# Attention layer, forward and gradients in one kernel: pairs of heads from head 32, eight fixed slot pairs and staging in single slots

## The chip, the cores and the metric

The kernel runs on one core of one Trainium2 chip. The metric is the device time of one execution in microseconds; the median of three runs before the change is 1707.09 us (1704.97 to 1707.36).

## What is computed

One decode step of a pre-LayerNorm block (cached attention, then a SwiGLU), and the gradients of its output for all inputs. B = 4 tokens, 32 heads, 4096 cached keys of 128 numbers; all tensors are bfloat16.

```python
def _A_ref(x, k_cache, v_cache, wq, wo):
    q = (x @ wq).reshape(B, Sq, H, Dh).transpose(0, 2, 1, 3)
    scores = jnp.einsum("bhqd,bhkd->bhqk", q, k_cache) * (Dh ** -0.5)
    p = _softmax(scores, axis=-1)
    o = jnp.einsum("bhqk,bhkd->bhqd", p, v_cache)
    return o.transpose(0, 2, 1, 3).reshape(B, Sq, H * Dh) @ wo
def _B_ref(x, w1, w3, w2):
    return (_silu(x @ w1) * (x @ w3)) @ w2

h = x + _A_ref(_layernorm(x), k_cache, v_cache, wq, wo)
h2 = h + _B_ref(_layernorm(h), w1, w3, w2)
# outputs: h2 and the gradients for x, k_cache, v_cache, wq, wo, w1, w3, w2
```

With 128 pairs of token and head, K, V, dK and dV have 134 MB each. For one query per head the gradients of the caches are outer products: dV = p dO^T and dK = dS q^T, with dS = p (V dO - c) / sqrt(128), where c is the product of dO and o. So the kernel reads K once, reads V twice (once for o, once more for V dO), writes dK and dV once, and does the small weight gradients beside it.

## The kernel before

The order of all instructions is written out by hand. Each engine works through its own instructions in that order, and all large transfers are issued by SyncE (SP), also in order.

**Slots.** Nearly all data goes through one SBUF tile, `arena`, cut into 23 slots of 4160 bfloat16 numbers per partition (`NSLOT`, `SLOT`). A head of K, V, dK or dV fills one slot (1 MB). `Slot` takes the slot that has been free longest (`free`, a queue); `give` puts it back when the code that used it has been written out. What then really waits on the chip is the next user of that slot: a load waits for the engines that read the old contents, and a computation that writes the slot waits for the store from it to land. `Slot2` takes two neighbouring slots for a pair of heads (2 MB, 16 KB per partition). In the last part of the kernel (`part["B"]`) `lone_slot` picks single slots at the ends of odd runs of free slots, and `Slot2.choices` lists the neighbouring pairs that are free in runs.

**Forward part.** By groups of two heads: scores, softmax, and a matrix from which o and part of dq come; K and V are loaded a few heads ahead. Eight slots, M, keep results of all 128 heads for the backward part. After it a short middle part does the SwiGLU forward and backward and loads V again, as many heads as slots are free.

**Backward part.** First heads one by one, from head `SP` = 24 in pairs of heads.
- `front(s)` (singles) and `front_pair(t)` (pairs): V is transposed by TensorE in groups of eight 128x128 blocks (L803, L1274) and evicted by ScalarE (L804, L1275) onto the same slot; matmuls with dO (L1208, L1289) give dP. After a group of heads `rows_out` and `rows_T` turn the result around, and `group_dS` or `group_dS_pair` (L1302, L1305, VectorE) makes dS.
- `grad_V`, `grad_K` (L820, L1232) and `grad_pair` (L1355, L1365): VectorE writes the outer product into a fresh slot or pair (2.3 us for a head at L809, 4.4 us for a pair at L1355), and SP stores it.
- `load_V2` (L836) and `load_pair` (L1257) load V ahead: `load_pairs` keeps up to three pairs loaded and not yet used. dV runs eight heads ahead of dK (`lead_V`), V's transposes three pairs ahead (`LP`).
- `side(s)` puts small work between the heads: up to head 20 what is left of dO (`rest_of_dO`), up to head 34 `dq_work`, which gives back an M slot after each 16 heads, and from head 35 two steps of `side_work` per head.
- `side_work` makes dq and dx (loading wq again by `load_wq2`), then the gradient of wq, then loads w2, makes the output h2 (its rows are put into slots `rows1`, `rows2`: ScalarE copies at L1096, a VectorE addition at L1111), and then the gradients of w2, w1, w3 and wo. A weight gradient is built by `grad_unit`: one matmul of 512 columns into PSUM, evicted by ScalarE at the next unit (L979).
- `staged` collects these units in a pair of slots and stores the pair (L1071) when it is full: seven stores of 1.8 or 2 MB. Halfway through a pair it takes the next one, so that for half of the time two pairs are held for staging.

The heart of the single and paired choice before the change:

```python
def __init__(self, name, src=free):          # Slot
    if src is free and part["B"]:
        lone_slot()
    self.i = src.popleft()
```

Of the kernel before, what the change touches and what calls it, by code (L numbers as in the profile page):

```python
# [18 lines left out]
NSLOT = 23  # L19
JQ = 8  # L20
NPE = 1
SP = 24


@with_exitstack
def kernel(
# [22 lines left out]
    nc = tc.nc  # L49
    P = nc.NUM_PARTITIONS  # L50

    B = A_x.shape[0]
    D = A_x.shape[-1]
    H = A_k_cache.shape[1]
    Sk = A_k_cache.shape[2]
    Dh = A_k_cache.shape[3]
    F = B_w1.shape[1]
    NH = B * H
    HD = H * Dh
    assert NH == P and Dh == P and H == 32 and Sk == 32 * P  # L60
    assert D == 4 * P and F % P == 0
    DC = D // P
    SJ = Sk // P
    FC = F // P
# [12 lines left out]
    f_chunks = []  # L77
# [27 lines left out]
    fcon = cF.enter_context(tc.tile_pool(name="fcon", bufs=1))  # L105

    free = deque(range(NSLOT))
    part = {"B": False}
    arena = slotp.tile([P, NSLOT * SLOT], BF16, name="arena")

    class Slot:
        def __init__(self, name, src=free):
            if src is free and part["B"]:
                lone_slot()
            self.i = src.popleft()
            self.t = arena[:, self.i * SLOT:(self.i + 1) * SLOT]

        def b(self, n=4096):
# [8 lines left out]
        def give(self):  # L127
            free.append(self.i)

    def runs_of_free():  # L130
        runs = []
        for i in sorted(free):
            if runs and runs[-1][-1] == i - 1:
                runs[-1].append(i)
            else:
                runs.append([i])
        return runs

    def lone_slot():
        at = {i: n for n, i in enumerate(free)}  # L140
        runs = runs_of_free()
        odd = [e for r in runs if len(r) % 2 for e in (r[0], r[-1])]
        i = min(odd or [e for r in runs for e in (r[0], r[-1])], key=lambda e: at[e])
        free.remove(i)
        free.appendleft(i)

    class Slot2:
        @staticmethod
        def choices():
            at = {i: n for n, i in enumerate(free)}  # L150
            return [(max(at[r[n]], at[r[n + 1]]), r[n]) for r in runs_of_free() for n in range(len(r) - 1)
                    if len(r) % 2 or n % 2 == 0]

        def __init__(self):
            self.i = min(self.choices())[1]
# [55 lines left out]
    for i in range(2):  # L211
        t = fcon.tile([P, 64], BF16, name=f"onesw{i}")
# [4 lines left out]
    def ones_window(col):  # L217
# [11 lines left out]
                          in_=rowg[:, None, :, None].to_broadcast([P, 4, 8, 4]))  # L229
# [70 lines left out]
    with ExitStack() as c0:  # L300
# [19 lines left out]
        for r in range(2):  # L320
            for t_ in range(2):
                for q in range(4):
                    nc.tensor.matmul(qr_ps[32 * q:32 * (q + 1), 2 * r + t_, :], lhsT=ident_b[:, 64 * r + t_:64 * (r + 1):2],
                                     rhs=qT_bf[:], start=True, stop=True, tile_position=(0, 32 * q))
# [204 lines left out]
    def two_slots(nm):  # L529
        return [Slot(nm + "a"), Slot(nm + "b")]  # L530
# [7 lines left out]
    def load_w2():  # L538
        sl = two_slots("w2")
        for i in range(2):  # L540
            nc.sync.dma_start(out=sl[i].b(7 * D).rearrange("p (c j) -> p c j", c=7),
                              in_=B_w2.rearrange("(p c) j -> p c j", c=FC)[:, i * 7:(i + 1) * 7, :])
        return sl
# [93 lines left out]
    units = {"d": d_hh_units()}  # L637
# [15 lines left out]
    for gi in range(NGI):  # L653
        nxt = gi < NGI - 1
        a, na, nb = gi * G, gi * G + 2, gi * G + 3
# [137 lines left out]
    V2s, VTs = {}, {}  # L793
# [38 lines left out]
    def load_V2(eng=nc.sync):  # L832
        s = nv["next"]
        if s < SP:
            V2s[s] = Slot("V2", vring if vring else free)
            eng.dma_start(out=V2s[s].heads(), in_=cache_head(A_v_cache, s))  # L836
            nv["next"] += 1

    with ExitStack() as cm:
# [70 lines left out]
        for sl in w1 + w3:  # L910
            sl.give()
        rs = Slot("reps")
        rep_bufs = {nm_: [rs.b()[:, (2 * k + i) * 512:(2 * k + i + 1) * 512].rearrange("p (i d) -> p i d", i=REP) for i in range(2)]
                    for k, nm_ in enumerate(("rq", "rdo"))}
        dh = rs.f(2080)[0:B, 1024:1024 + D]
# [50 lines left out]
    with ExitStack() as c2:  # L966
# [9 lines left out]
        def grad_flush():  # L976
            if gu:
                dst, ps, n = gu.pop()
                nc.scalar.copy(out=dst, in_=ps[:, 0:n])  # L979


        def grad_unit(dst, lhsT, rhs):
            n = rhs.shape[-1]
            ps = psg.tile([P, 512], FP32, tag="gps", name="gps")
            nc.tensor.matmul(ps[:, 0:n], lhsT=lhsT, rhs=rhs, start=True, stop=True)
            grad_flush()
            gu.append((dst, ps, n))
# [23 lines left out]
        def side_work():  # L1011
# [4 lines left out]
            t = rs.f(2080)[:, 1536:1536 + NH]  # L1016
# [6 lines left out]
            flat = Slot("dqflat")  # L1023
# [7 lines left out]
            for cc in range(DC):  # L1031
                wq2 = wq2s.popleft()
# [19 lines left out]
            xhat_bf = fs.t[0:B, 6 * D:7 * D]  # L1052
# [5 lines left out]
            nc.vector.tensor_tensor(out=dx_bf, in0=dh, in1=lnbx, op=ALU.add)  # L1058
            nc.gpsimd.dma_start(out=o1_2, in_=dx_bf)
            yield  # L1060
            stage = deque([Slot2()])

            def staged(units, out_ap):
                st = stage.popleft()
                for n, (a, w_, lhsT, rhs) in enumerate(units):
                    if n == len(units) // 2:
                        stage.append(Slot2())
                    grad_unit(st.t[:, a:a + w_], lhsT, rhs)
                    yield
                grad_flush()  # L1070
                nc.sync.dma_start(out=out_ap, in_=st.t[:, 0:out_ap.shape[-1]])  # L1071
                st.give()

            for i in range(2):
                if i == 1:
                    w2 = load_w2()
                yield from staged([(r * HD + n8 * 512, 512, xhat_bf[0:B, 2 * P * i + r:2 * P * (i + 1):2],
                                    flat.b(HD)[0:B, n8 * 512:(n8 + 1) * 512]) for r in range(2) for n8 in range(HD // 512)],
                                  out_4[2 * P * i:2 * P * (i + 1), :].rearrange("(p r) n -> p (r n)", r=2))
            flat.give()  # L1080
            fs.give()

            r1, r2 = Slot("rows1"), Slot("rows2")
            hh_rows, dg_rows, du_rows = r1.t[0:B, 0:F], r1.t[0:B, F:2 * F], r2.t[0:B, 0:F]
            gr_bf, dh_bf, hhat_bf = r1.t[0:B, 2 * F:2 * F + D], r2.t[0:B, F:F + D], r2.t[0:B, F + D:F + 2 * D]
# [21 lines left out]
            for sl in w2:  # L1107
# [3 lines left out]
            nc.vector.tensor_tensor(out=h2_bf, in0=hrows, in1=o2_ps[0:B, :], op=ALU.add)  # L1111
            nc.gpsimd.dma_start(out=o0_2, in_=h2_bf)
            yield
            hw = hh_rows.rearrange("b (p k) -> b k p", k=FC)
            yield from staged([(k * D, D, hw[:, k, :], gr_bf) for k in range(FC)],
                              out_8.rearrange("(p k) j -> p (k j)", k=FC))
            oflat = Slot("oflat")
            for b in range(B):
                nc.gpsimd.dma_start(out=oflat.b(HD)[b:b + 1, :], in_=O_sb[b::B, :])
            nw = hhat_bf.rearrange("b (p k) -> b k p", k=DC)  # L1120
            for (rows, out_ap) in ((dg_rows, out_6), (du_rows, out_7)):
                yield from staged([(k * F + f0_, w_, nw[:, k, :], rows[:, f0_:f0_ + w_]) for k in range(DC) for (f0_, w_) in f_chunks],
                                  out_ap.rearrange("(p k) f -> p (k f)", k=DC))
            r1.give()
            for h0 in range(0, H, 16):
                ow = oflat.b(HD)[0:B, h0 * P:(h0 + 16) * P].rearrange("b (p k) -> b k p", k=16)
                yield from staged([(k * D, D, ow[:, k, :], dh_bf) for k in range(16)],
                                  out_5[h0 * P:(h0 + 16) * P, :].rearrange("(p k) j -> p (k j)", k=16))
            stage.popleft().give()
            oflat.give()  # L1130
            r2.give()

        units["s"] = side_work()


# [29 lines left out]
        rows = {}  # L1165
# [5 lines left out]
        def dO_window(s):  # L1171
            if s < SP:
                nc.gpsimd.tensor_copy(out=zd[s % B][:, 32:132:67], in_=dOT_bf[:, s:s + 1].to_broadcast([P, 2]))

        def P_pairs(s):
            if s < SP and s not in P2s:
                P2s[s] = bw3.tile([P, SJ, 2], BF16, tag="P2", name="P2")
                nc.gpsimd.tensor_copy(out=P2s[s][:], in_=P_all[:, s, :, None].to_broadcast([P, SJ, 2]))
# [13 lines left out]
        def front(s):  # L1192
# [20 lines left out]
            sl = VTs.pop(s)  # L1213
            (vring if nv["next"] < SP and len(V2s) + len(VTs) + len(vring) < NV2 else free).append(sl.i)

# [19 lines left out]
        def prefetch():  # L1235
            while nv["next"] < SP and vring:
                load_V2(nc.sync)


        NT = (NH - SP) // 2  # L1240
        H0 = SP // B
        pV, pP2, pdS, psl = {}, {}, {}, {}
        npv = {"next": 0}
# [9 lines left out]
        def load_pair():  # L1253
            t = npv["next"]
            npv["next"] += 1
            pV[t] = Slot2()
            nc.sync.dma_start(out=pV[t].t[:, 0:2 * SJ * Dh], in_=two_heads(A_v_cache, t))  # L1257

        def load_pairs(t):
            while npv["next"] < NT and (npv["next"] <= t or len(pV) < 3 and len(Slot2.choices()) > 1):  # L1260
                load_pair()

        def dO_pair(t):
# [44 lines left out]
        Pp, zt, P2b = {}, [], []  # L1308
# [189 lines left out]
```

## Time and profile before

| | |
|---|---|
| span of the profiled execution | 1707.2 us |
| busy: PE, DVE, ACT, POOL | 73%, 72%, 56%, 18% |
| bytes moved, mean rate | 707.45 MB, 414 GB/s |
| read from HBM, written to HBM | 422.59 MB, 282.34 MB |
| stores of 2 MB, median time to landing | 108, 21.2 us |
| loads of V by pairs, median time to landing | 52, 24.6 us |
| matmul clock granted, mean | 0.845 |

A reader of this profile should look at stretches of time and not at totals. The shares of PE, DVE and ACT are averages over a forward part (to about 655 us), a middle part (to about 715 us) and a backward part, which use the engines differently; the rate of the DMA engines in 40 slices shows where the transfers run at their best and where they do not. "Time to landing" is the time from a transfer's issue until its last piece has arrived, so it includes the time spent in the queue: a long one means that much work stands in front of it. A wait in the waits view names the engine and line that waited, what it waited for, and then the microseconds in total, the number of waits and the longest.

### The profile page before, as it was taken

To read this page: it belongs to the slowest core of one execution; us is meant where nothing else is said; L and a number is where in the kernel's file an instruction comes from. 1 tells how busy PE (TensorE), PEld (TensorE's weight loads), DVE (VectorE), ACT (ScalarE), POOL (GpSimd) and SP (SyncE) were. 2 spreads that over 40 slices of the span, in tenths; PEclk is the share of its full clock that TensorE was granted. 3 is DMA by queue.
4 is the path that set the end of the run, shared out by engine and by line. 5 is a ranking of instruction groups with operands and counts; after the bars stand their busy time and mean duration, and the time that the engine had idled before them with its cause. 6 is when DMAs were issued, how large, how long until landed. Compare 5 with 4: busy or idle time off the path is not lost. (4 is left out here: it accounts for less than half of the span.)

```text
span 1707.2 us, 37798 instructions
## 1 busy us (share of the span) xinstructions
PE 1247.2 (73%) x16232; PEld 959.9 (56%) x16232; DVE 1232.0 (72%) x1190; ACT 958.9 (56%) x1489; POOL 314.0 (18%) x575
## 2 busy tenths in 40 slices
PE   5889888888888888878776666577557665766642
PEld 4777776767676767656565555445334443444431
DVE  5989999999999986667396665665555565555574
ACT  3555444544454444676576576567557665756541
POOL 1211222223222321223003020012103011011010
PEclk9999999999999999798888788866668666767685
DMA  9999999999999999999999999999999999999997
GB/s 401 424 425 424 424 423 425 424 424 423 414 423 412 424 406 401 379 424 425 421 375 427 428 425 428 429 429 430 427 413 428 412 411 403 407 413 406 399 402 336
DMA packets 78264, 707.45 MB, mean 414 GB/s; under 512 B 8444, under 2 KB 12680, under 8 KB 14224
## 3 DMA queue, kind: packets, MB, share of 16 engines
q1 hardware_dynamic: 77680, 704.94, 99.1%
q8 instruction: 127, 2.08, 0.5%
q14 instruction: 41, 0.34, 0.0%
q0 software_dynamic: 416, 0.10, 0.0%
HBM read 422.59 MB, written 282.34 MB: 413 GB/s over the span
## 5 line engine op out<-in xcount | busy, mean ns | idle before, releaser
L1275 ACT COPY arena<-pt_tps 128x1024 bf16<-128x1024 bf16 x416 | 400.4, 1023 | 243.3 <-PE pt_tps L1274 243.0
L1274 PE MATMUL pt_tps<-ident_b,arena 128*128 128x128 bf16 x3328 | 333.9, 272 | 220.8 <-DMA arena<-in_A_v_cache_dram 148.8
L1274 PEld LDWEIGHTS <-arena 128*128 128x128 bf16 x3328 | 288.0, 126 | 323.7 <-DMA arena<-in_A_v_cache_dram 174.6
L1355 DVE TENSOR_TENSOR arena<-arena 128x8192 bf16<-128x8192 bf16 x52 | 229.9, 4421 | 163.4 <-DMA out_dram<-arena 161.9
L1355 DVE TENSOR_TENSOR arena<-dS,arena 128x8192 bf16<-128x8192 bf16 x52 | 230.0, 4426 | 131.8 <-DMA out_dram<-arena 131.8
L475 PE MATMUL M_ps<-arena 128*128 128x130 bf16 x4096 | 286.6, 222 | 37.5 <-DMA arena<-in_A_v_cache_dram 37.1
L460 DVE TENSOR_TENSOR arena<-arena 128x4096 bf16<-128x4096 bf16 x128 | 292.5, 2285 | 24.9 <-POOL arena L456 24.9
L475 PEld LDWEIGHTS <-arena 128*128 128x128 bf16 x4096 | 253.8, 99 | 58.4 <-DMA arena<-in_A_v_cache_dram 50.5
L367 DVE STREAM_TRANSPOSE arena<-arena 128x512 f32<-128x512 f32 (+1 forms) x321 | 250.6, 797 | 0.0
L362 ACT COPY arena<-pt_tps 128x1024 bf16<-128x1024 bf16 x128 | 129.4, 1012 | 186.8 <-PE pt_tps L361 150.3
L1352 POOL COPY arena<-arena 128x128 bf16<-128x128 bf16 x52 | 71.5, 1376 | 598.2 <-DVE arena L1355 380.8
L373 POOL TENSOR_TENSOR W<-qrep,wmask 128x128 bf16<-128x128 bf16 x128 | 120.5, 941 | 85.6 <-PE S_ps L393 70.7
L456 POOL COPY arena<-P_all 128x64 bf16<-128x64 bf16 x128 | 32.4, 253 | 413.8 <-ACT P_all L450 410.8
L804 ACT COPY arena<-pt_tps 128x1024 bf16<-128x1024 bf16 x96 | 91.7, 1026 | 18.3 <-PE pt_tps L803 17.0
L1289 PE MATMUL dP_ps<-arena 128*32 128x512 bf16 x832 | 92.2, 474 | 9.8 <-ACT arena L1275 9.5
L450 ACT COPY P_all<-pt_P 32x64 bf16<-32x64 bf16 x256 | 51.9, 203 | 55.3 <-PE pt_P L446 53.0
L803 PE MATMUL pt_tps<-ident_b,arena 128*128 128x128 bf16 x768 | 64.2, 242 | 24.6 <-ACT arena L804 20.4
L361 PE MATMUL pt_tps<-ident_b,arena 128*128 128x128 bf16 x1024 | 80.5, 223 | 0.0
L485 PE MATMUL kP_ps<-arena,onesw 128*32 128x512 bf16 x1024 | 79.2, 386 | 0.0
L809 DVE TENSOR_TENSOR arena<-dS,arena 128x4096 bf16<-128x4096 bf16 x24 | 55.0, 2297 | 30.2 <-DMA out_dram<-arena 29.9
L361 PEld LDWEIGHTS <-arena 128*128 128x128 bf16 x1024 | 62.0, 100 | 25.9 <-issue 25.8
L393 PE MATMUL S_ps<-arena,W 128*32 128x256 bf16 x1536 | 75.2, 285 | 0.5 <-DVE arena L367 0.2
(245 smaller groups left out, 1503.4 us busy)
## 6 DMA issues: line engine op xcount, KB each, us to landing
out_dram<-arena SPq DMA_DIRECT2D x108, 2048.0 KB, 21.2
arena<-in_A_v_cache_dram SPq DMA_DIRECT2D x152, 1024.0 KB, 15.7
arena<-in_A_k_cache_dram SPq DMA_DIRECT2D x128, 1024.0 KB, 15.5
arena<-in_A_v_cache_dram SPq DMA_DIRECT2D x52, 2048.0 KB, 24.6
out_dram<-arena SPq DMA_DIRECT2D x48, 1024.0 KB, 12.5
arena<-in_A_wq_dram SPq DMA_DIRECT2D x8, 1024.0 KB, 18.0
arena<-in_B_w_dram SPq DMA_DIRECT2D x8, 896.0 KB, 15.2
out_dram<-arena SPq DMA_DIRECT2D x3, 1792.0 KB, 25.2
```

The costliest lines, as they stand in the source:

```text
L361: nc.tensor.transpose(pt[:, i, :], Kn[:, c * GW + i, :], ident_b[:])
L362: nc.scalar.copy(out=KT[:, c * GW:(c + 1) * GW, :], in_=pt[:])
L367: nc.vector.transpose(out=KT[:, c * w_:(c + n) * w_], in_=Kn[:, c * w_:(c + n) * w_])
L373: nc.gpsimd.tensor_tensor(out=W[:, hl], in0=qrep[:, :, s:s + 1].to_broadcast([P, 4, 32]), in1=wmask[:, hl, None, :].to_broadcast([P, 4, 32 ...
L460: nc.vector.tensor_tensor(out=PK[:, :, 0:Dh].rearrange("p j (r t) -> p j r t", t=2), in0=Ks[s].heads().rearrange("p j (r t) -> p j r t", t=2),
L475: nc.tensor.matmul(hold["M"][:], lhsT=Vn[:, j, :], rhs=PK[:, j, :], start=(j == 0), stop=(j == SJ - 1))
L485: nc.tensor.matmul(hold["kP"][32 * q:32 * (q + 1), :, :], lhsT=ones_window(w), rhs=PK[:, j0:j0 + 4, 0:Dh], start=(w == 0 and c == 0), stop ...
L804: nc.scalar.copy(out=v[:, g * GW:(g + 1) * GW, :], in_=pt[:])
L1274: nc.tensor.transpose(pt[:, i, :], v[:, g * GW + i, :], ident_b[:])
L1275: nc.scalar.copy(out=v[:, g * GW:(g + 1) * GW, :], in_=pt[:])
L1289: nc.tensor.matmul(rows["acc"][32 * c:32 * (c + 1), :], lhsT=zt[t % B][:, 32 - m:64 - m], rhs=v[:, j0:j0 + 4, :], start=(pl == 0 and u == ...
L1355: nc.vector.tensor_tensor(out=dst.rearrange("p (j r t) -> p j r t", r=Dh // 2, t=2), in0=col2[:, :, None, :].to_broadcast([P, 2 * SJ, Dh / ...
```

## The change

1. Pairs begin at head 32 instead of 24 (`SP`), so the backward part has 48 pairs and not 52.
2. After the slot `reps` is taken, the first eight even-aligned slot pairs that do not hold it are fixed as `part["pairs"]`. Pairs for V, dV and dK come only from these, until the side work is done; then from all aligned pairs. `runs_of_free` and `lone_slot` go.
3. The slots of side work (`SIDE`: P by pairs, wq, dq, rows, o, staging) come from the seven slots outside the fixed pairs.
4. Weight gradients are staged in one slot each: 14 stores of 0.9 or 1 MB. The layout of the rows in DRAM changes with it: 7 or 8 KB in one piece per partition.
5. w2 is loaded after the gradient of wq and not in its middle. `load_pairs` counts single V heads that are loaded too.

The purpose is that the pairs that carry the large transfers are never taken for staging, and that pairs begin when the M slots have been given back.

```diff
-SP = 24
+SP = 32
+NPAIR = 8
...
-    part = {"B": False}
+    part = {"B": False, "side_done": False}
+    SIDE = ("Pp", "wq2", "dqflat", "fin", "rows1", "rows2", "oflat", "w2a", "w2b", "gwq", "gw2", "gw13", "gwo")
...
-            if src is free and part["B"]:
-                lone_slot()
-            self.i = src.popleft()
+            if name in SIDE and part["B"]:
+                self.i = next(i for i in free if i not in part["pairs"])
+                free.remove(self.i)
+            else:
+                self.i = src.popleft()
...
-            return [(max(at[r[n]], at[r[n + 1]]), r[n]) for r in runs_of_free() for n in range(len(r) - 1)
-                    if len(r) % 2 or n % 2 == 0]
+            return [(max(at[i], at[i + 1]), i) for i in (range(0, NSLOT - 1, 2) if part["side_done"] else sorted(part["pairs"])[::2])
+                    if i in at and i + 1 in at]
...
         rs = Slot("reps")
+        kept = [i for i in range(0, NSLOT - 1, 2) if rs.i not in (i, i + 1)][:NPAIR]
+        part["pairs"] = {j for i in kept for j in (i, i + 1)}
...
-            stage = deque([Slot2()])
-
-            def staged(units, out_ap):
-                st = stage.popleft()
-                for n, (a, w_, lhsT, rhs) in enumerate(units):
-                    if n == len(units) // 2:
-                        stage.append(Slot2())
-                    grad_unit(st.t[:, a:a + w_], lhsT, rhs)
+            for cc in range(DC):
+                st = Slot("gwq")
+                for n8 in range(HD // 512):
+                    grad_unit(st.b(HD)[:, n8 * 512:(n8 + 1) * 512], xhat_bf[0:B, cc * P:(cc + 1) * P],
+                              flat.b(HD)[0:B, n8 * 512:(n8 + 1) * 512])
                     yield
                 grad_flush()
-                nc.sync.dma_start(out=out_ap, in_=st.t[:, 0:out_ap.shape[-1]])
+                nc.sync.dma_start(out=out_4[cc * P:(cc + 1) * P, :], in_=st.b(HD))
                 st.give()
...
             flat.give()
             fs.give()
+            w2 = load_w2()
...
+            part["side_done"] = True
...
-            while npv["next"] < NT and (npv["next"] <= t or len(pV) < 3 and len(Slot2.choices()) > 1):
+            while npv["next"] < NT and (npv["next"] <= t or len(V2s) + 2 * len(pV) < 6 and len(Slot2.choices()) > 1):
```

The staging loops of the gradients of w2 (two slots), w1 and w3 (two each) and wo (four) are changed in the same way as that of wq (four).

More of the change, by code (lines that the diff above doesn't have):

```diff
@@ L128, in give @@
             free.append(self.i)
[L130 to L145, printed above, removed]
     class Slot2:
@@ L1060, in side_work @@
             yield
-            stage = deque([Slot2()])
-            def staged(units, out_ap):
-                st = stage.popleft()
-                for n, (a, w_, lhsT, rhs) in enumerate(units):
-                    if n == len(units) // 2:
-                        stage.append(Slot2())
-                    grad_unit(st.t[:, a:a + w_], lhsT, rhs)
+            for cc in range(DC):
[3 more added lines that the diff above has]
+                              flat.b(HD)[0:B, n8 * 512:(n8 + 1) * 512])
                     yield
                 grad_flush()
-                nc.sync.dma_start(out=out_ap, in_=st.t[:, 0:out_ap.shape[-1]])
+                nc.sync.dma_start(out=out_4[cc * P:(cc + 1) * P, :], in_=st.b(HD))
                 st.give()
[L1074 to L1079, printed above, removed]
             flat.give()
             fs.give()
+            w2 = load_w2()
             r1, r2 = Slot("rows1"), Slot("rows2")
@@ L1113, in side_work @@
             yield
-            hw = hh_rows.rearrange("b (p k) -> b k p", k=FC)
-            yield from staged([(k * D, D, hw[:, k, :], gr_bf) for k in range(FC)],
-                              out_8.rearrange("(p k) j -> p (k j)", k=FC))
+            for i in range(2):
+                st = Slot("gw2")
+                hw = hh_rows[:, i * 7 * P:(i + 1) * 7 * P].rearrange("b (p k) -> b k p", k=7)
+                for k in range(7):
+                    grad_unit(st.b(7 * D)[:, k * D:(k + 1) * D], hw[:, k, :], gr_bf)
+                    yield
+                grad_flush()
+                nc.sync.dma_start(out=out_8[i * 7 * P:(i + 1) * 7 * P, :].rearrange("(p c) j -> p c j", c=7),
+                                  in_=st.b(7 * D).rearrange("p (c j) -> p c j", c=7))
+                st.give()
             oflat = Slot("oflat")
@@ L1119, in side_work @@
                 nc.gpsimd.dma_start(out=oflat.b(HD)[b:b + 1, :], in_=O_sb[b::B, :])
-            nw = hhat_bf.rearrange("b (p k) -> b k p", k=DC)
             for (rows, out_ap) in ((dg_rows, out_6), (du_rows, out_7)):
-                yield from staged([(k * F + f0_, w_, nw[:, k, :], rows[:, f0_:f0_ + w_]) for k in range(DC) for (f0_, w_) in f_chunks],
-                                  out_ap.rearrange("(p k) f -> p (k f)", k=DC))
-            r1.give()
[L1125 to L1129, printed above, removed]
+                for i in range(2):
+                    st = Slot("gw13")
+                    nw = hhat_bf[0:B, i * 2 * P:(i + 1) * 2 * P].rearrange("b (p k) -> b k p", k=2)
+                    for k in range(2):
+                        for (f0_, w_) in f_chunks:
+                            grad_unit(st.b(2 * F)[:, k * F + f0_:k * F + f0_ + w_],
+                                      nw[:, k, :], rows[:, f0_:f0_ + w_])
+                            yield
+                    grad_flush()
+                    nc.sync.dma_start(out=out_ap[i * 2 * P:(i + 1) * 2 * P, :].rearrange("(p c) f -> p c f", c=2),
+                                      in_=st.b(2 * F).rearrange("p (c f) -> p c f", c=2))
+                    st.give()
+            r1.give()
+            for h0 in range(0, H, 8):
+                st = Slot("gwo")
+                ow = oflat.b(HD)[0:B, h0 * P:(h0 + 8) * P].rearrange("b (p k) -> b k p", k=8)
+                for k in range(8):
+                    grad_unit(st.b(8 * D)[:, k * D:(k + 1) * D], ow[:, k, :], dh_bf)
+                    yield
+                grad_flush()
+                nc.sync.dma_start(out=out_5[h0 * P:(h0 + 8) * P, :].rearrange("(p k) j -> p k j", k=8),
+                                  in_=st.b(8 * D).rearrange("p (k j) -> p k j", k=8))
+                st.give()
             oflat.give()
             r2.give()
+            part["side_done"] = True
         units["s"] = side_work()
```

## The prediction

> **What bounds the kernel now.** I read the page's parts 2 and 3 first. DMA is the only row that is full in every slice, and one queue holds it.
>
> ```profile
> DMA  9999999999999999999999999999999999999997
> GB/s 401 424 425 424 424 423 425 424 424 423 414 423 412 424 406 401 379 424 425 421 375 427 428 425 428 429 429 430 427 413 428 412 411 403 407 413 406 399 402 336
> q1 hardware_dynamic: 77680, 704.94, 99.1%
> ```
>
> The 704.94 MB are the same after the change, so time can only come from the rate. Up to slice 29 it is near 425 with a few dips; then it stays near 408. The windows view cuts the backward part where it changes (columns: stretch, its length, busy us of PE, PEld, DVE, ACT, POOL, PE clock, DMA share, GB/s):
>
> ```profile
> 848.00:898.00 50.00, 39.07 (x444) 30.58 (x444) 43.05 (x32) 32.58 (x40) 5.03 (x8) 0.83 0.93 377
> 898.00:1225.00 327.00, 214.37 (x2195) 161.07 (x2195) 200.37 (x106) 202.83 (x241) 51.76 (x48) 0.76 1.01 428
> 1300.00:1325.00 25.00, 17.73 (x156) 11.87 (x152) 14.65 (x9) 16.99 (x23) 4.55 (x2) 0.70 1.01 431
> 1325.00:1650.00 325.00, 204.96 (x1758) 143.16 (x1756) 187.03 (x90) 192.67 (x246) 32.98 (x43) 0.68 1.00 408
> 1650.00:1707.00 57.00, 16.85 (x168) 12.67 (x168) 34.94 (x18) 16.21 (x18) 0.00 (x0) 0.65 0.84 345
> ```
>
> No compute engine is full from 898 on (DVE, the busiest beside ACT, is at 58 to 61%), so the question is what keeps the DMA engines from their best rate. The waits view (us in total, times, longest), then the timeline of SP's queue (start, us from the first to the end of the last):
>
> ```profile
> DVE arena L1355 <- DMA out_dram<-arena: 293.7, 54, 12.2
> ACT arena L1096 <- DMA out_dram<-arena: 14.7, 1, 14.7
> ```
>
> ```profile
> 1054.85 5.43 SPq L1365 DMA_DIRECT2D out_dram<-arena  x2
> 1060.38 0.78 SPq L1257 DMA_DIRECT2D arena<-in_A_v_cache_dram  x1
> ...
> 1439.52 4.67 SPq L1365 DMA_DIRECT2D out_dram<-arena  x2
> 1444.28 0.67 SPq L1257 DMA_DIRECT2D arena<-in_A_v_cache_dram  x1
> 1449.86 9.96 SPq L1365 DMA_DIRECT2D out_dram<-arena  x2
> ```
>
> DVE waits for a slot pair whose last store has not landed. Buffers therefore set how many bytes stand in the queue. L1365's time to landing, asked by window, says how many: median 25.6 us in 900 to 1225, 20.3 in 1225 to 1650 (in 1439 to 1451: 16.2).
>
> [...] the last store (issued at 1688.5) lands first on one engine at 1697.5, last at 1706.2. Between a transfer's first and last completion step lie 2.4 us at 923, 4.2 at 1018, 6.1 at 1103, 9.0 at 1227: a nearly constant lead grows by some 2.2 us per 100 us. [...]
>
> **The account.** A slot comes free when the slowest engine has landed, and the run ends with that engine, so I count on its clock. The transfers issued after the 1 MB store of 841.4 (landed 15.1 later, 856.5) are 350.2 MB. That engine lands the last of them at 1706.2: 849.7 us, 412 GB/s. From the store issued at 882.9 (lands 15.5 later, 898.4) to the one of 1211.7 (lands 20.2 later, 1231.9) lie 140.2 MB in 333.5 us: 420.4 GB/s, its rate when nothing starves. At that rate 350.2 MB take 833.0, so 16.7 us are lost, in two places: 856.5 to 898.4 moved 15.7 MB, worth 37.4, in 41.9 (lost 4.5); 1231.9 to the end moved 194.2 MB, worth 462.1, in 474.3 (lost 12.2).
>
> Why there? I compared slots in the two programs: bytes that stand in the queue between a slot's last transfer and its next. In before's 898 to 1160, stores have 10.5 to 11.5 MB and V loads 23 to 25 MB: four pairs go round for V, four for gradients. From the first staging pair on, stores fall to 8.4 and then often 6.3 MB, and V loads too, as they take the pair that a store has just left. 6.3 MB are 15 us of the slow engine; a store needs 4.4 of them for DVE, and the fastest engine is 9 us ahead: it has 2 us of work left at issue. 10.5 MB leave 25 - 4.8 = 20.2 us less the lead. In 1300 to 1325 the lead is as large (9 us) but the fastest engine reaches each transfer 6 us or more after its issue, and the rate is 431. So I read the dips as an empty queue on the fast engines, not as the lead itself. At the transition (848 to 898) slots are worse: single-head gradients reuse a slot after 2.1 to 4.2 MB because load_pairs took three pairs while the M slots were still held; DVE idles 10.2 us to 851.5 and then runs full.
>
> **The change part by part.**
> - SP 24 to 32: four fewer pairs; eight heads go singly, in 24 transfers of 1 MB for 12 of 2 MB. DVE: 16 outers of 2.29 (L809) for 8 of 4.42 (L1355): +1.3 us in 60 us of DMA, hidden under DMA, DVE has slack. Transfers: 25 MB at 420 GB/s (window 715 to 848) for 428: +1.1 us in mean rate; on the slow engine I take +0.7.
> - Transition moved to where M is nearly all returned (given back by about head 34). In the changed program the smallest distance there is 5.2 MB (12.4 us; less 4.4 DVE, 1 issue, 4 lead leaves some 3 us), then 7.3 and up. Saved: 4.5, bounds 1.5 to 4.5.
> - Eight fixed pairs and staging in single slots: stores now have 10.5 to 11.5 MB all the way, V loads 23 to 27. That is before's own state of 898 to 1160, held to the end. Saved: up to 12.2. But the lead is no longer cut: from about 4 at 850 it could reach 4 + 2.2 x 8.4 = 22 us, when 20.2 to 22.6 are in reserve. Late stalls cost 0 (if a stop earlier cuts the lead) to 4 us (2.6% of the last 150); I take 1.
> - Staging in 14 single stores for 7: the same 82 matmuls (gps, 0.43 us) and as many evictions (0.60), hidden; 13.6 MB at 420 for 428: 0.3 us.
> - A longer wait: rows1 takes slot 22, just stored by the last gwq transfer. ACT's copy (L1096, now L1076) waits for that store. Before it waited 14.7; now the store is issued about 6 us after V of the same iteration lands and 35 us of bytes after that V have to land: about 26. Behind it on ACT stand the four last transposes of that pair, then two pairs' copies, the rows' transposes and o2; DVE waits for o2 (7.6 before) ahead of the next dV. From the landing to that DVE operation are 24 ACT copies, 24 us plus hand-overs, 31 in all, and 4.4 for dV: issued 36 us after, while the slow engine has bytes for 34. It loses 2 plus start-up, I take 3 (0 to 6); fast engines lose some 10 and with them their lead.
>
> Sum: 1707.2 - 16.7 + 0.7 + 0.3 + 1 (late) + 3 (rows1) = 1695.5, less than 1 either way for the transition; I say 1695.
>
> **Rivals.**
> A, the low rate of 1325 to 1650 belongs to the weight gradients or to the lead itself, not to the short queue. For: it starts with them. Against: 431 at 1300 to 1325, with both present. Then 12.2 stay: 1707.2 - 4.5 + 1 = 1703.7.
> B, slower: eight fixed pairs leave no spare (before has room for nine beside reps, Pp, dqflat and two wq2), the transition is only moved (nothing gained), the 12.2 stay, and the 11 us that the rows1 wait grows by are exposed: 1707 + 11 = 1718; with half of it 1712. For: a full in-order ACT stop of 26 us exceeds the 20 us reserve. Against: two stores are ready without ACT in it.
> C, a middle: the late lead brings the stalls back from 1500 on, and rows1 costs 6: about 1701.
>
> **How the numbers follow.** Forecast 0.62 (1689 to 1699), C 0.18, A 0.10, B 0.10. Without any loss the sum gives 1690.5; a slightly better rate of the slow engine, 1688: that is the low end. The high end of 1705 takes in C and A. Faster by over 0.2% (under 1703.7): forecast, C and a third of A, 0.84; same 0.06; slower 0.10.
>
> **What would show it.** GB/s of 425 or more from 900 to about 1600; no slice near 375 at the transition; L1365 to landing 24 us or more in the second half; one ACT wait of about 26 us and a DVE wait for o2 in 1230 to 1290, with one dip there; at the end fast engines done 10 us or more ahead. Wrong if the rate falls to 408 while the time to landing is over 24 (A), or if DVE or PE waits appear that are not for DMA (B).

## The result, and the profile after

| | before | after |
|---|---|---|
| median of 4 executions each | 1707.22 us (1704.97 to 1710.17) | 1698.65 us (1697.27 to 1699.82) |
| ratio, 95% interval | | 0.9948 (0.9931 to 0.9966) |
| span of the profiled execution | 1707.2 us | 1696.6 us |
| time of that same execution | 1709.01 us | 1698.35 us |

The changed kernel is 8.6 us faster by the medians and 10.6 us by the two profiled spans; the forecast was 12 us. The time of an execution is 1.8 us above its span in both kernels, and the profiled execution of before was 1.9 us above the median of 1707.09 from which the forecast started.

Parts 2, 3 and 6 of the page of the changed kernel, with the rows that were shown of before:

```profile
DMA  9999999999999999999999999999997999999998
GB/s 400 424 425 423 424 423 425 424 424 424 416 422 413 424 402 400 391 411 425 426 426 426 416 427 429 430 429 429 430 423 309 418 425 426 429 428 430 429 429 343
q1 hardware_dynamic: 80416, 704.94, 99.0%
out_dram<-arena SPq DMA_DIRECT2D x96, 2048.0 KB, 27.7
```

The bytes are the same. The slice of 375 GB/s at the transition is gone and the last third is near 429 instead of 408; there is one new hole, slice 31 with 309. The windows view of the changed kernel (columns: stretch, its length, busy us of PE, PEld, DVE, ACT, POOL, PE clock, DMA share, GB/s):

```profile
848.00:898.00 50.00, 39.69 (x439) 29.52 (x440) 27.35 (x24) 34.11 (x41) 15.39 (x14) 0.93 1.01 426
898.00:950.00 52.00, 37.54 (x395) 29.01 (x393) 33.80 (x16) 30.97 (x38) 12.42 (x6) 0.85 1.01 417
950.00:1250.00 300.00, 191.74 (x1924) 141.09 (x1922) 189.84 (x105) 183.55 (x220) 37.33 (x41) 0.74 1.01 429
1250.00:1350.00 100.00, 61.07 (x630) 40.37 (x629) 57.42 (x28) 66.74 (x84) 24.75 (x24) 0.78 0.90 371
1350.00:1650.00 300.00, 198.67 (x1703) 137.75 (x1704) 187.39 (x90) 185.69 (x236) 21.40 (x34) 0.67 1.01 428
1650.00:1697.00 47.00, 9.66 (x89) 6.96 (x88) 15.84 (x9) 8.27 (x10) 0.00 (x0) 0.63 0.81 348
```

The waits view of the changed kernel (us in total, times, longest) names the hole, and the timeline of ScalarE (start, us from the first to the end of the last, and in brackets the idle time before) shows what stood behind it:

```profile
DVE arena L1357 <- DMA out_dram<-arena: 243.1, 74, 14.2
ACT arena L1076 <- DMA out_dram<-arena: 28.9, 1, 28.9
DVE arena L1091 <- PE o_ps L1086: 14.5, 1, 14.5
```

```profile
1237.45 0.59 ACT L968 CAST arena<-gps 128x512 bf16<-128x512 f32 x1
1266.98 0.89 ACT L1076 COPY arena<-pt_Tr 4x896 bf16<-4x896 bf16 x1 [28.94 <-DMA out_dram<-arena]
1267.79 1.90 ACT L1277 COPY arena<-pt_tps 128x1024 bf16<-128x1024 bf16 x2
```

ScalarE stops for 29 us for the slot of `rows1`, with the V transposes of the next pairs (L1277) behind it. DVE still waits long for slots to land (243 us), but a store now has a median of 27.6 us from issue to landing after 1225 us, where it had 20.3: when a store is issued, more bytes stand ahead of it.

All comparisons below use one clock, the one of the prediction: the moment at which the slowest of the 16 DMA engines has landed a given number of megabytes. It is read from the last of a transfer's 16 completion steps; which engine that is, the trace does not say. The lead is the time from a transfer's first completion step to its last, that is how far the fastest engine is ahead of the slowest. That each step stands for one engine is a reading of the trace: in the kernel before, from 900 to 1650 us, 16 packets of q1 are under way 84% of the time (mean 16.0), and at the end it is a single one from 1699.5 us, when 15 steps of the last store are in, until the 16th comes at 1706.2. DVE's waits of over 0.1 us for a landing end at the 16th step, 78 of 79 in the kernel before and 94 of 94 in the changed one.

| MB landed | before, us | after, us | difference | lead before | lead after |
|---|---|---|---|---|---|
| 370 | 897.4 | 894.4 | -3.0 | 2.0 | 5.8 |
| 400 | 968.0 | 966.9 | -1.1 | 3.1 | 6.0 |
| 520 | 1253.9 | 1253.8 | -0.1 | 7.9 | 14.3 |
| 550 | 1326.2 | 1327.5 | +1.3 | 9.4 | 2.0 |
| 580 | 1399.6 | 1400.7 | +1.1 | 8.8 | 5.4 |
| 640 | 1547.9 | 1542.0 | -5.9 | 9.6 | 7.4 |
| 704.9 | 1706.2 | 1695.3 | -10.9 | 8.8 | 10.2 |

Up to 580 MB the change has brought nothing that lasted. The whole gain lies in the last 125 MB.

### The profile page after: what moved, and what is told of

Same layout as the page of the kernel before. It is cut to its first block, busy times and chain, and to the rows that moved or that the text cites. A ratio compares the mean times of both kernels' runs of the same rounds, so it can differ in the third digit from the quotient of the medians.

```text
span 1696.6 us, 37845 instructions
## 1 busy us (share of the span) xinstructions
PE 1245.9 (73%) x16228; PEld 953.4 (56%) x16228; DVE 1234.4 (73%) x1198; ACT 959.0 (57%) x1490; POOL 329.5 (19%) x583
## 5 line engine op out<-in xcount | busy, mean ns | idle before, releaser
L1277 ACT COPY arena<-pt_tps 128x1024 bf16<-128x1024 bf16 x384 | 369.5, 1024 | 208.4 <-PE pt_tps L1276 208.0
L1276 PE MATMUL pt_tps<-ident_b,arena 128*128 128x128 bf16 x3072 | 309.7, 273 | 205.5 <-DMA arena<-in_A_v_cache_dram 124.1
L1276 PEld LDWEIGHTS <-arena 128*128 128x128 bf16 x3072 | 266.1, 126 | 307.2 <-issue 154.9
L1357 DVE TENSOR_TENSOR arena<-arena 128x8192 bf16<-128x8192 bf16 x48 | 212.3, 4424 | 255.6 <-DMA out_dram<-arena 223.7
L462 PEld LDWEIGHTS <-arena 128*128 128x128 bf16 x4096 | 253.6, 99 | 58.7 <-DMA arena<-in_A_v_cache_dram 51.7
L1357 DVE TENSOR_TENSOR arena<-dS,arena 128x8192 bf16<-128x8192 bf16 x48 | 212.4, 4427 | 19.6 <-DMA out_dram<-arena 19.4
L1354 POOL COPY arena<-arena 128x128 bf16<-128x128 bf16 x48 | 38.8, 808 | 501.9 <-ACT arena L1331 276.3
L790 PE MATMUL pt_tps<-ident_b,arena 128*128 128x128 bf16 x1024 | 82.1, 236 | 25.5 <-ACT arena L791 25.5
L1291 PE MATMUL dP_ps<-arena 128*32 128x512 bf16 x768 | 86.0, 484 | 7.8 <-ACT arena L1277 7.6
L790 PEld LDWEIGHTS <-arena 128*128 128x128 bf16 x1024 | 70.8, 108 | 36.1 <-issue 34.9
L796 DVE TENSOR_TENSOR arena<-P,arena 128x4096 bf16<-128x4096 bf16 x29 | 66.3, 2296 | 20.1 <-DMA out_dram<-arena 19.7
L348 PE MATMUL pt_tps<-ident_b,arena 128*128 128x128 bf16 x1024 | 80.5, 223 | 0.0
L796 DVE TENSOR_TENSOR arena<-dS,arena 128x4096 bf16<-128x4096 bf16 x32 | 73.5, 2302 | 6.6 <-DMA out_dram<-arena 6.2
```

The source lines that it names most:

```text
L462: nc.tensor.matmul(hold["M"][:], lhsT=Vn[:, j, :], rhs=PK[:, j, :], start=(j == 0), stop=(j == SJ - 1))
L790: nc.tensor.transpose(pt[:, i, :], v[:, g * GW + i, :], ident_b[:])
L796: nc.vector.tensor_tensor(out=dst.rearrange("p j (r t) -> p j r t", t=2), in0=col2[:, :, None, :].to_broadcast([P, SJ, Dh // 2, 2]), in1=r ...
L1276: nc.tensor.transpose(pt[:, i, :], v[:, g * GW + i, :], ident_b[:])
L1277: nc.scalar.copy(out=v[:, g * GW:(g + 1) * GW, :], in_=pt[:])
L1291: nc.tensor.matmul(rows["acc"][32 * c:32 * (c + 1), :], lhsT=zt[t % B][:, 32 - m:64 - m], rhs=v[:, j0:j0 + 4, :], start=(pl == 0 and u == ...
```

## The experiments

Theory at the start: the rate falls when too few bytes lie between two uses of a slot for the fast engines to find work, so eight pairs and single-slot staging bring the gain. Rivals: the low rate belongs to the weight gradients, or the later start brings the gain. For the comparisons the kernel before ran beside these kernels too: 90 executions with a median of 1707.6 us, from 1697.1 to 1712.9, 13 of them under 1701. So about one execution in seven of the kernel before is nearly as fast as the changed kernel; none of these was profiled. That spread turns out to matter.

### Fewer pairs

```diff
-NPAIR = 8
+NPAIR = 7
```

> The changed kernel with seven fixed pairs for eight and nothing else changed: staging, layouts, head 32 and side work stay. In the built program the stores of pairs then have 8 to 9 MB between two uses of a pair (10.5 to 13 before) and V loads 8 to 9 (23 to 27). Theory (the queue on the fast engines must not run dry): 8.6 MB are 20.5 us of the last engine, less 4.8 for VectorE leave 15.7, so the queue of the fastest engine runs dry when the lead passes about 13 us, near 1200 us of the run; after that the rate falls below 425 and the lead stops growing. About 1703 us, 4 to 5 slower than the changed kernel. Rival (single-slot staging itself makes the gain): 1698 to 1699 us, and 428 GB/s to the end.

```diff
-NPAIR = 8
+NPAIR = 6
```

> The changed kernel with six fixed pairs. Stores of pairs then have 6 to 7 MB between uses, like the kernel before in its second half, but from the first pair on. Theory: 6.3 MB leave 15 - 4.8 = 10 us less the lead; the lead is 7 at 1000 us, so the stalls begin there and hold for 700 us: 410 GB/s or less from 1000 to 1650, the lead no larger than 9, about 1713 us, slower than both kernels. Rival (single-slot staging itself makes the gain): near 1699. Rival (the low rate belongs to the weight gradients): 428 up to 1140, lower after.

Measured: with seven pairs 1702.64 us (1700.53 to 1705.17), ratio 0.9977 (0.9963 to 0.9991); with six 1716.34 us (1715.70 to 1718.51), ratio 1.007 (1.004 to 1.0101). The theory had 1703 and 1713. Windows of the kernel with six pairs, then of the one with seven:

```profile
950.00:1250.00 300.00, 183.55 (x1970) 133.83 (x1969) 182.03 (x104) 188.59 (x227) 31.57 (x45) 0.79 1.01 421
1250.00:1350.00 100.00, 63.62 (x576) 43.41 (x576) 54.66 (x25) 59.98 (x76) 10.23 (x17) 0.76 1.00 402
1350.00:1650.00 300.00, 188.49 (x1624) 131.06 (x1624) 176.67 (x86) 178.41 (x228) 18.57 (x35) 0.70 1.00 403
```

```profile
950.00:1250.00 300.00, 189.96 (x1976) 138.00 (x1974) 184.36 (x105) 190.07 (x228) 69.97 (x46) 0.78 1.01 428
1250.00:1350.00 100.00, 68.88 (x576) 46.23 (x576) 57.27 (x28) 60.51 (x76) 17.55 (x17) 0.67 1.00 420
1350.00:1650.00 300.00, 192.47 (x1660) 135.49 (x1661) 182.72 (x85) 181.10 (x231) 66.40 (x35) 0.68 1.00 415
```

With six pairs the rate is below 429 already between 950 and 1250 us. Between 1066 and 1100 it is 415, where the changed kernel has 430; the first matmul of a weight gradient starts only at 1118 and the first store of one is issued at 1147. So the weight gradients are not the cause. The lead grows as in the changed kernel up to 1058 us (8.5 us); at 1142 it is 8.0, and 11.1 in the changed kernel. What the number of pairs sets is how far the engines drift apart in these runs. The slot that a store needs must first land on the slowest engine, and then comes DVE's work (4.4 us for a pair). So I estimate that the fastest engine can be ahead by the bytes between the two uses, in time of the slowest engine (its 420.4 GB/s), less the 4.8 us that the prediction allowed from landing to issue (4.5 by the median of both profiles, before and after). Counting those bytes for the stores in each built program gives:

| kernel | smallest usual distance of stores | ceiling of the lead, worked out | lead seen once it stopped growing |
|---|---|---|---|
| six pairs | 6.3 MB | 15.0 - 4.8 = 10.2 us | 6.8 to 11.3 (1060 to 1670 us) |
| before, second half | 6.3 MB | 10.2 us | 7.6 to 10.4 (1254 to 1670 us) |
| seven pairs | 8.4 MB, from 560 MB on 9.3 | 20.0 - 4.8 = 15.2 us, then 17.3 | 13.9 to 18.0 (1285 to 1670 us) |
| rows slot taken early (below) | 11.4 to 11.5 MB | 22.3 to 22.6 us | 20.3 to 21.6 (1505 to 1670 us) |

The levels follow the distances; single values lie up to 3.4 us under the rule and up to 1.2 us over it. In all of these the slowest engine loses speed as well once the lead stands at the ceiling, although it still has the length of the lead, some 7 to 21 us, of work in front of it when the fastest has none: it moves 402 GB/s with six pairs, 405 in the kernel before and 415 with seven pairs (550 to 680 MB), and 417 with the rows slot taken early (625 to 680 MB), where its rate when nothing starves was 420.4. That the distance between uses limits the lead is shown; why the slowest engine pays for it is not.

### The start at head 24

```diff
-SP = 32
+SP = 24
```

> The changed kernel with pairs from head 24 again: fixed pairs and single-slot staging without the later start. In the built program single-head gradients near the transition have 5 to 12 MB with one V load at 2, and pairs have 8 to 9 until about 420 MB, then 10.5 to 13 as in the changed kernel. Theory: the second half gains all of what it gains in the changed kernel (about 11 us on the last engine from 1400 us on); the transition keeps the loss of before, 2 us net of what the changed kernel gained there. 1700 to 1702 us. Rival (head 32 makes the gain): 1705 to 1707.

Measured: 1701.10 us (1697.94 to 1702.21), ratio 0.9967 (0.9954 to 0.9980), 428 GB/s from 1350 to 1650. The slots alone, without the later start, bring 6.5 of the 9 us; the later start adds 2.5 to them by the medians. But that 2.5 does not lie at the transition: in the two profiles this kernel's slowest engine is 0.6 us ahead of the changed kernel's at 580 MB and 2.8 behind at the end. From 440 to 680 MB the distances of the two are the same, so these do not explain it either.

### The later start alone

The kernel before, with one edit:

```diff
-SP = 24
+SP = 32
```

> The kernel before with its transition at head 32 in place of head 24, and nothing else: still a rotating pool of slots, weight gradients still staged as before. In its order of uses the slots at the new transition still come back after only 2 to 4 MB, and those of the second half after 6 to 8 MB. Theory (the bytes between two uses of a slot set the rate, the head is only where it happens): 1705 to 1708 us, the same as before; about 408 GB/s from 1350 to 1650 us, the fast DMA engines no further ahead than in the kernel before. Rival (the later transition itself makes the gain, because fewer heads run in the backward part by pairs): 1699 to 1701 us and 425 GB/s or more from 1350 to 1650 us.

Measured: 1699.80 us, ratio 0.9963 (0.9951 to 0.9976). The rival's number came, not that of the theory: the later start alone, with the old pool of slots, brings 7.8 us. The transition itself does not bring it: up to 550 MB nothing is gained (1326.5 us in its first profile, 1326.2 in the kernel before), and the dip has only moved (371 GB/s from 898 to 950). Each part alone brings most of the gain, so the two gains overlap. Two findings bear on it. First, I had written that the distances of this kernel stay at 6 to 8 MB. Counted again, they do so only up to about 627 MB (1510 us); from there they are 8 to 10, where the kernel before stays at 6 to 8 up to about 680 MB. Second, the executions of this one program lie from 1697.64 to 1708.89 us. Three further profiles of it:

> The kernel of e5 once more (before with the transition at head 32, nothing else), for a further profile of it: its 20 runs lay from 1697.6 to 1708.9 us, and the first profile was of a short one (span 1696.1 us). Theory (the distance of 6 to 8 MB is on the edge, so the same program goes either way by where the DMA engines stand to each other when the second half begins): a long run has the same waits and the same order, but 405 to 415 GB/s from 1350 to 1650 us, with all the engines but the last bunched together; a short run again has 424 GB/s. Rival (long runs come from something else, such as the granted clock or a stall in the first half): the second half has 424 GB/s in long runs too.

> As the one before, a third profile of the kernel of e5. Theory: a span of 1696 to 1700 us with 420 GB/s or more from 1350 to 1650 us, or one of 1702 to 1707 us with 405 to 416 GB/s there; nothing of the difference before 1250 us. Rival: a difference that lies before 1250 us, or none of the rate.

> As the two before, a fourth profile of the kernel of e5. Theory: the span and the rate from 1350 to 1650 us go together, 10 us of span for every 13 GB/s or so. Rival: they don't.

Their spans were 1696.0, 1702.1 and 1697.8 us (the first profile: 1696.1). Windows of the kernel before, then of the short execution of 1696.0 us, then of the long one of 1702.1 us:

```profile
1350.00:1540.00 190.00, 122.83 (x1045) 85.74 (x1044) 107.20 (x48) 116.98 (x153) 19.06 (x22) 0.68 1.00 409
1540.00:1650.00 110.00, 63.06 (x562) 44.80 (x560) 63.23 (x34) 59.06 (x73) 10.56 (x11) 0.69 0.99 408
```

```profile
1350.00:1540.00 190.00, 129.93 (x1075) 87.21 (x1073) 114.85 (x55) 120.63 (x158) 25.15 (x23) 0.66 1.01 422
1540.00:1650.00 110.00, 65.41 (x611) 48.13 (x612) 71.01 (x33) 63.85 (x77) 15.04 (x11) 0.71 1.01 429
```

```profile
1350.00:1540.00 190.00, 122.68 (x1061) 85.00 (x1060) 110.16 (x53) 118.83 (x155) 25.23 (x24) 0.69 1.00 413
1540.00:1650.00 110.00, 63.95 (x586) 45.52 (x585) 69.69 (x30) 61.22 (x76) 16.16 (x11) 0.72 1.01 429
```

The same program moves 422 or 413 GB/s where its distances are 6 to 8 MB, and 429 both times where they are 8 to 10. On the clock of the slowest engine the long execution is behind the short one by 1.6 us at 550 MB (it was 1.8 already at 340), by 6.1 at 640 and by 6.1 at the end: 4.5 us of the 6.1 are lost between 550 and 640 MB and nothing after. So the theory holds for the place of most of the difference, but not for "nothing before 1250 us"; and over 1350 to 1650 us the long execution has 419 GB/s against 425 in the short one, not the 405 to 416 that were forecast. The span of 1697.8 goes with 424 GB/s over 1350 to 1650; its 1.8 us above the shortest lie before 340 MB again (2.1 there). The kernel before, at 6 to 8 MB for longer, loses another 5.2 us against the long execution from 625 MB to the end.

So 6 to 8 MB are an edge in these executions: with a lead of 8 to 10 us the queue held in one and didn't in the other. In the short execution the lead stood at 8.0 to 8.8 us between 1390 and 1545 us without loss for the slowest engine (420.7 GB/s from 550 to 640 MB), in the long one at 8.0 to 10.0 with one (412.1). A difference goes with it: in the short execution, at 1540 us, the 15 other engines are spread over 2.8 to 8.6 us ahead of the slowest, in the kernel before, at 1542, they stand bunched at 7.5 to 9.3, and in the long execution they lie between (4.4 to 8.8). What decides it at about 1350 us is not shown.

### The stop of ScalarE taken away

`rows1` is taken before the staging of the gradient of wq, and the sources of that gradient are given back before the last of its slots; the rows then get a slot that is not about to be stored.

```diff
+            r1 = Slot("rows1")
             for cc in range(DC):
                 st = Slot("gwq")
...
+                if cc == DC - 1:
+                    flat.give()
+                    fs.give()
                 st.give()
-            flat.give()
-            fs.give()
             w2 = load_w2()
...
-            r1, r2 = Slot("rows1"), Slot("rows2")
+            r2 = Slot("rows2")
```

> The changed kernel with rows1 taken before the gradient of wq is staged, and the slots of dq and fin given back before the last staged slot, so that ScalarE's first copy into rows1 (a wait of 28.9 us in the changed kernel) finds a slot without a store in flight. Theory: this wait and the dip at 1250 to 1350 go (4.3 us on the last engine between 1289 and 1401), but the lead of the fast engines is not cut there and reaches 18 us and more by 1500, so that the queue runs dry late and 0 to 3 us come back: 1695 to 1697 us. Rival (the wait is hidden by the queue and the dip is only fast engines idling): 1698 to 1699.

Measured: 1698.61 us (1697.49 to 1701.40), ratio 0.9954 (0.9937 to 0.9971), the same as the changed kernel. The number is the rival's; the hole went and the queue ran dry late, as the theory said, but more came back than 0 to 3 us. Its windows:

```profile
1250.00:1350.00 100.00, 69.01 (x586) 46.44 (x584) 58.36 (x28) 61.26 (x77) 14.02 (x19) 0.70 1.01 429
1350.00:1500.00 150.00, 101.72 (x862) 70.01 (x861) 87.63 (x44) 96.97 (x128) 14.08 (x18) 0.68 1.01 428
1500.00:1650.00 150.00, 92.15 (x829) 66.34 (x828) 99.67 (x46) 88.11 (x109) 8.04 (x15) 0.70 1.01 419
1650.00:1697.00 47.00, 9.01 (x89) 6.25 (x88) 15.40 (x9) 8.17 (x10) 0.00 (x0) 0.64 0.58 248
```

The stop and the hole are gone, and at 610 MB the slowest engine is 4.8 us ahead of where the changed kernel has it. At the end it is 0.5 ahead. Without the hole nothing pulls the engines together: the lead grows from 14.6 us at 1254 to 21.0 at 1505, meets the ceiling, and from there the rate is 419 instead of 429. In the changed kernel the hole costs the slowest engine about 4 us and cuts the lead from 14.3 to 2.0, so that it ends at 10.2 and never meets the ceiling. By the medians both ways cost the same.

The ceiling explains only part of this. From 580 MB to the end the slowest engine takes 298.5 us here and 294.6 in the changed kernel, but 298.0 in the kernels with the start at head 24 and at head 40, which have the hole too. So the late stalls cost some 0.5 us against those two. The other 3.4 belong to the profiled execution of the changed kernel: between 580 and 655 MB its slowest engine moves faster than in these kernels, while its fastest engine keeps the same distance in time to theirs. There is one profile of it, and the reason is open.

### The start at head 40

```diff
-SP = 32
+SP = 40
```

> The changed kernel with its transition at head 40 in place of head 32, the eight pairs and seven single slots kept. The smallest distances at the transition become about 6 MB instead of 5 MB, the others stay at 10 MB or more. Theory (the transition of the changed kernel still costs 1 to 2 us on the last DMA engine): 1697 to 1699 us, the dip of 928 to 945 us moved and smaller. Rival (the later start leaves too little for the singles, and the loss moves elsewhere): 1700 us or more.

The same edit together with that of the rows:

> Two edits on the changed kernel together: the row work's slot taken before the staging of the query weight gradient (so that ScalarE doesn't wait 29 us for it), and the transition at head 40. Theory (what is gained in the middle lets the fast DMA engines run further ahead, and the queue then runs dry late, as with the first of these edits alone): 1697 to 1699 us, the rate above 428 GB/s to about 1500 us and below 425 after it. Rival (the two gains add up): 1693 to 1695 us.

Measured: head 40 alone 1701.15 us (1698.68 to 1703.03), ratio 0.9966 (0.9954 to 0.9977); both edits 1699.44 us (1698.55 to 1700.77), ratio 0.9953 (0.9942 to 0.9965). Windows of the kernel with both:

```profile
898.00:950.00 52.00, 26.52 (x272) 19.69 (x270) 25.95 (x16) 20.98 (x24) 6.16 (x6) 0.76 1.01 426
950.00:1250.00 300.00, 203.20 (x2074) 147.84 (x2073) 187.29 (x108) 199.11 (x240) 52.37 (x51) 0.76 0.99 418
1350.00:1500.00 150.00, 102.86 (x857) 71.77 (x858) 88.10 (x44) 95.11 (x124) 12.30 (x18) 0.66 1.01 429
1500.00:1650.00 150.00, 91.66 (x827) 66.14 (x827) 97.84 (x46) 88.56 (x111) 9.53 (x15) 0.70 1.01 429
```

Head 40 alone is 2.5 us slower than the changed kernel by the medians: the rival of its expectation came. The dip of 898 to 950 is gone, but it comes back larger before 1250 us (418 instead of 429): it has moved with the transition, and a distance of 6 MB is again not enough for a lead of 7.6 us. "Smaller" was wrong. With both edits I had expected the queue to run dry late; it doesn't, since the larger dip cut the lead to 1.8 us at 1005 us and it reaches only 19.8 at the end. Against the edit of the rows alone, the slowest engine falls from 0.7 us behind at 370 MB to 2.6 behind at 415, and is 2.0 behind at the end. So there are not two gains that could add up. With the start at head 40, though, taking the stop away brings 1.7 us by the medians.

## Why the prediction was right, and where it wasn't

The direction and most of the size came out, and of the two places one. That the sum came so close is partly luck. On the clock of the slowest engine it had 3.8 us (4.5 - 0.7) saved before the second loss begins, and at 520 MB only 0.1 were; it had 7.9 (12.2 - 0.3 - 1 - 3) for the rest, and 10.8 came. The two errors have opposite signs. By the steps of the prediction:

- **What bounds the kernel.** Right: one queue, and the rate went with the bytes in front of a store. 428 GB/s from 1350 to 1650 and 27.6 us to landing were named as signs (425 or more, 24 or more), and six pairs, with 6.3 MB between stores, brought the low rate back (403).
- **Transition, saved 4.5 (1.5 to 4.5).** The mechanism was right, the size was not. 3.0 us were saved by 370 MB, but 1.1 are left at 400, 0.8 at 490 and 0.1 at 520: most of it goes to a dip that the changed kernel has of its own (417 GB/s in 898 to 950). The term at fault is "less 4 lead leaves some 3 us" for the distance of 5.2 MB: the lead there was 7.3 us, so nothing was left. The fastest engine reached the store issued at 928.2 only 0.4 us after its issue.
- **Fixed pairs and staging, saved up to 12.2.** Right in mechanism and place: 12.0 us between 580 MB and the end. Of these 8.6 also come with the start at head 24, whose transfers have the same distances there; the other 3.4 are those of the one profiled execution (above). And fixed pairs are not the only way to it, as the prediction's split between the parts said: the later start alone also leads to longer distances at the end.
- **The lead, 22 us at most, late stalls 1.** The drift was as forecast in size: without the hole 14.6 us at 1254 and 21.0 at 1505, 2.5 per 100 us (forecast 2.2). In the changed kernel the late stalls were 0; the hole came first and cut the lead.
- **The stop for `rows1`.** Forecast a wait of about 26 us, measured 28.9. Forecast a loss of 3 us (0 to 6): from 520 to 580 MB the slowest engine took 146.9 us, at 420.4 GB/s it would be 142.7, so 4.2 were lost. What the sum lacked is that little of this loss is left at the end: the experiment without the stop ends only 0.5 us earlier, though its late stalls explain but a small part of that.
- **The base.** The sum started from the span of 1707.2 and its result was called the time. From span to span it gave 1695.5, and 1696.6 was measured. So of the 3.7 us by which 1695 missed 1698.65, 1.1 are an error of the sum, 1.8 the time outside the span, 0.5 the rounding down, and 0.3 the profiled execution against the median. Three figures of it were misread, without weight for the sum: the staging has 110 matmuls in all (82 are those after 1225 us) and 13.9 MB, not 13.6, and the busiest compute engine from 898 to 1225 us was PE with 66%.
- **Rivals.** A fell with the six pairs, and with the 429 GB/s of the changed kernel up to 1250 us at a lead of up to 14.3 us; B fell with the result. C (1701) had the right thing in it, a lead that meets the ceiling late, but it happens only without the stop.

## What to carry to other kernels

In a kernel bound by one DMA queue, count for each buffer the bytes that pass between two uses of it; turned into time, less the work from landing to issue, this had to exceed here the distance by which the DMA engines had drifted apart, and not only the work (10.2 us by that count and a lead of 7.6 to 10.4 went with 405 GB/s in the kernel before). Near that edge one program took from 1697.64 to 1708.89 us, so look at the spread of executions and not at one profile; a difference of 3.4 us between single profiles of this case had no cause that the program shows. The stall here, in which the slow engine caught up from 14.3 to 2.0 us, was not lost altogether: it cost 4.2 us at its place, and without it the end came 0.5 us earlier. Before taking one away, look whether the queue is deep enough for the drift that follows.

## What was not expected of the hardware

In these runs the 16 DMA engines of one queue drift apart by 2.2 to 2.5 us in 100 us for long stretches (from 2.4 to 9.0 us between 923 and 1227 us in the kernel before, from 14.6 to 21.0 between 1254 and 1505 with the rows slot taken early), up to 21.6 us, and the lead fell clearly where the rate dipped (from 14.3 to 2.0 us in the hole of the changed kernel). When the fast ones ran dry, the slowest lost speed too although it had work: its 60 MB from 1326 to 1473 us took 147.3 us in the kernel before, against 142.7 at its undisturbed 420.4 GB/s. It did not always: in the short execution above it lost nothing while the lead stood still at 8.0 to 8.8 us. In the kernel before one engine is alone at the end: from 1250 to 1690 us the last but one is 4.0 to 8.7 us ahead of it, and at 594 MB the fifteen others were 6.4 to 10.0 us ahead. In the changed kernel, from 1400 to 1680 us, the last but one is only 0.1 to 2.4 us ahead. What makes one engine slower than the others, and why it loses speed with them, stays open: the records of packets do not tell the engines apart.
